# Clustered attention and a bilinear layer on one core: an eleventh sorted pair of heads, and rows that carry their pair's number

## The chip, the core and the metric

The program runs on one core of a Trainium2 chip. A core has five engines with a queue of instructions each: PE (matrix products, into the accumulator memory PSUM), DVE (vector operations), ACT (activations and copies), POOL (here it issues indirect transfers, in which a list of indices says which rows go where) and SP (here it issues plain transfers). Each engine runs its queue in order; they meet through semaphores. The metric is the device time of one execution in microseconds (us).

## The reference

```python
# q, k, v: (4, 8, 768, 64); centroids: (8, 16, 64)
q_assign = argmax(q_n @ c_n.T); k_assign = argmax(k_n @ c_n.T)     # nearest of 16 centroids
mask = q_assign[:, :, :, None] == k_assign[:, :, None, :]
scores = where(mask, scale * q @ k.T, -1e9)
attn = softmax(scores) @ v                                       # (4, 8, 768, 64)
x = attn.transpose(0, 2, 1, 3).reshape(3072, 512)
out = ((x @ w_a) * (x @ w_b)) @ w_out                            # 512 -> 1536 -> 512
```

A query attends only to the keys of its own cluster. The weights arrive as float64 bit patterns and are rounded to float32 in the kernel.

## The kernel before

**Pairs.** Two heads of one batch make a pair; there are 16 pairs, four for each batch, numbered p = 0 to 15. The first `ND` = 6 pairs are *dense*: every score of 768 x 768 is computed, and a large negative term, added by a one-hot product, pushes pairs of other clusters out. A dense pair has 12 units (two halves of queries, six blocks of keys); `score` (line 592) makes the scores of two units, `add_up` (623) sums their exponentials on DVE, `weigh` (634) multiplies them with v, `denominators` (654) and `normalize` finish a half. Pairs 4 and 5 are prepared *by blocks*: DVE turns q and k (514), PE makes similarities (405), DVE makes one-hot rows, and `move_one_hot` (496) moves them with eight transfers.

The other ten pairs are *sorted*, numbered n = 1 to 10 (p = ND + n - 1). Their rows of q, and of k beside v, are written to memory in the order of clusters, so that scores are needed only inside a cluster's strip. A sorted pair passes this chain, written out in `sorted_pair`:

1. *Load* rows (1313) or, for n above `EARLY` = 5, blocks (1324), queries (1332) and keys with values (1338), all on SP.
2. *Turn and assign*: PE transposes (1356) or, late, DVE (1346); similarities (1367) and a prefix count (1404, 1406) on PE; `find`, seven steps on DVE that end in the list of places (1458); `after`, four steps on DVE (1463 to 1472), of which three compute how many rows each cluster strip holds (`in_order`).
3. *Put*: 24 indirect transfers on POOL (1509), 12 of q rows into `qd`, 12 of k and v rows into `kvd`, a ring of five rooms that SP clears with zeros beforehand (`clear`, 1282).
4. *Reload* on SP (1539, 1543), into single buffers `sq`, `sk`, `v`. It waits for the previous pair's values.
5. *Turns* (1552) and *masks* (1557 to 1569) on DVE: from the counts a column of ones and zeros is made beside v, and rows that were not filled are multiplied by zero.
6. *Scores* (1581), exponentials (1592), *values* (1606, 1615), division (1625), and `keep` (1635), which writes the result to memory.
7. *Get*: 12 indirect transfers on POOL (1646), which bring the rows back into the order of tokens; `x_across` (1661) turns them on PE into the input of the bilinear layer.

Pairs 1 to 5 are indexed and put early, while the dense pairs run. Everything from the reload on needs the room that the dense stage leaves (`late_room`, once the dense stage is over and `after` of pair 5 is done).

**The bilinear layer** runs batch by batch. Batch 0's begins beside the last dense pairs, in two blocks of 384 tokens: the up products with `w_a` and `w_b` (727), the product of both on DVE (784), and the down products with `w_out`. Its second block overwrites rows of early pairs, so its first half waits for the puts of pair 3, its second half for those of pair 5. Batches 1 to 3 form all seven products of a two by two split in place of eight; `combine_x` (830) makes differences of x first, other differences (864, 1003, 1014) come in between. A batch's products start only when the last of its four pairs is turned.

**The weights** come in 36 parts: SP loads a part into one of two `raw` buffers (300), DVE rounds it with five instructions (311 to 329), ACT checks it with two (325, 326). The first eight have fixed places, the others are planned by `next_round`.

**The planner.** The order of instructions on each queue is fixed when the program is built, by a planner that keeps a clock for each engine (`Clocked`, with a cost for each kind of instruction) and a heap of due steps. A step of a chain is put off while its engine's clock is ahead of the planned time by more than a limit: `ATT` for turns and masks, `FRONT` for indexing, `LOADS` and `RELOAD` for SP. `paced` ties each indirect transfer to an instruction of PE so that they come `SPACE` apart. `arrived` notes when a weight part is thought to be there.

Of the kernel before, what the change touches and what calls it, by code (L numbers as in the profile page):

```python
# [157 lines left out]
def short_path(nc, tc, ctx, c, cn, centroids_in, casts, n_far, q, k, v,  # L158
# [8 lines left out]
    ND = 2 * HP - 2  # L167
# [5 lines left out]
    SPACE, EARLY, RING = 1.8, 5, 5  # L173
    FRONT, ATT, LOADS, RELOAD = 2.2, 2.8, 1.0, 3.0
# [7 lines left out]
    Gi = Clocked(nc.gpsimd, "G", 1.28, *state)  # L182
    Q_, Qr, Qc = (Clocked(nc.sync, "P", us, *state) for us in (0.42, 0.62, 2.0))
# [9 lines left out]
    counts = pool("counts", 5)  # L193
# [298 lines left out]
    def move_one_hot():  # L492
        while to_move:
            p, ohT, kq, a = to_move.popleft()
            r = 32 * kq + a * NC
            Qr.dma_start(out=ohTs[p][a * D:a * D + NC, kq * HB:(kq + 1) * HB],
                         in_=ohT[r:r + NC, :])
# [258 lines left out]
    def ffn_block(b, blk):  # L756
# [14 lines left out]
        def piece_a(f):  # L771
# [5 lines left out]
            box["h"] = early[blk].rearrange("p (f t) -> p f t", f=NF)  # L777
# [358 lines left out]
    ROWS = 1280  # L1136
    kvd = [dram.tile([2 * ROWS + 32, 2 * D], FP32, name=f"kvd{n}") for n in range(RING)]
# [5 lines left out]
    place = zero.tile([P, 2], FP32, name="place")  # L1143
    order_of = zero.tile([P, NC], FP32, name="order_of")
# [9 lines left out]
    ROW = 2 * NJ * 3 * D  # L1154

    def rooms(rows, qkT, temp, kk):
# [3 lines left out]
        R_["blocks"] = [t[:, 2 * NJ * D:ROW] for t in rows]  # L1160
# [6 lines left out]
    def sorted_constants():  # L1167
# [10 lines left out]
        ints = extra[:, P:P + 32].bitcast(INT32)  # L1178
        nc.gpsimd.iota(ints[:, 0:NC], pattern=[[1, 2], [2, NC // 2]], base=0,
                       channel_multiplier=0)  # L1180
        nc.gpsimd.iota(ints[:, NC:NC + 1], pattern=[[0, 1]], base=0,
                       channel_multiplier=1)
        V.tensor_copy(out=order_of, in_=ints[:, 0:NC])
        V.tensor_copy(out=place[:, 0:1], in_=ints[:, NC:NC + 1])
        Vs.tensor_copy(out=place[0:D, 1:2], in_=place[0:D, 0:1])
        V.tensor_scalar(out=place[D:P, 1:2], in0=place[D:P, 0:1],
                                scalar1=-float(D), scalar2=None, op0=ALU.add)

    def early_room():
        t = hp_.tile([P, NF * HB], FP32, name="h")  # L1190
# [83 lines left out]
    def clear(n):  # L1274
# [3 lines left out]
        def part(i):  # L1278
            t, x, w, m = (kvd[n % RING], 20, 2 * D, 5) if i < 4 else (
# [19 lines left out]
    def sorted_pair(n, start):  # L1299
# [7 lines left out]
        def load_rows(a, second):  # L1307
# [3 lines left out]
                    ((k, kvr[:, a, :, 0:D]), (v, kvr[:, a, :, D:])))[second]  # L1311
# [104 lines left out]
        def index():  # L1416
# [3 lines left out]
            sums, keys = room_[8][:, 0:G], room_[9]  # L1420
# [6 lines left out]
            def totals():  # L1427
# [3 lines left out]
                Vs.tensor_copy(out=keys, in_=total[:, 1])  # L1431
# [20 lines left out]
            def places():  # L1452
# [7 lines left out]
                M["idx"] = idx.rearrange("p (w j a) -> p w j a", w=2, j=NJ)  # L1460

# [7 lines left out]

            def in_order():  # L1470
                M["cnt"] = counts.tile([P, E], FP32, name="cnt_s")
                Vm.tensor_reduce(out=M["cnt"],
                                  in_=cmp.rearrange("p a c d -> p (a c) d"),
                                  axis=AX.X, op=ALU.add)
                mark("after", n)
# [18 lines left out]
                lambda: Vm.tensor_tensor(  # L1494
                    out=cmp, in0=halves(rank_of)[:, :, None, :].broadcast_to(shape),
                    in1=order_of[:, None, :, None].broadcast_to(shape),
                    op=ALU.is_equal),
                lambda: Vm.tensor_tensor(
                    out=cmp, in0=cmp,
                    in1=halves(keys)[:, :, None, :].broadcast_to(shape), op=ALU.mult),  # L1500
                in_order,
# [728 lines left out]
```

## Time and profile before

| What | us |
|---|---|
| median of three runs | 952.77 (952.34 to 955.7) |
| the profiled execution, device time | 951.85 |
| its span, first to last instruction | 950.1 |

The page of the profile gives busy time by engine, the chain of work that ended last, and groups of instructions by source line: output and input by the program's names, shape, count, busy us and mean ns, and the idle time of the engine before them with what ended it. A timeline row has start and duration in us, engine, line, operation, names, and in brackets an idle time before it with its releaser. A row of busy time by window has the window, its length, and for each engine busy us and the number of instructions, then the granted PE clock, the share of the transfer engines, and GB/s. Matmuls overlap at their ends, so the duration of a merged row is a little longer than its distance to the next.

### The profile page before, as it was taken

Reading aid. Unit: us, or ns where it says so; the run is one execution under the profiler, and the core shown is the slowest. Engines: PE = TensorE matmul, PEld = TensorE weight load, DVE = VectorE, ACT = ScalarE, POOL = GpSimd, SP = SyncE. Lnnn points to the kernel's source line nnn. Section 1 sums busy time; section 2 is a strip of 40 time slices with the busy share of each in tenths; the row PEclk is TensorE's granted clock in tenths of the full one; section 3 lists DMA queues with packets and bytes.
Section 4 is the critical chain, followed back from the end, with each engine's and each line's share of the span. In section 5 each row is a group of like instructions: output and inputs, shape, how many; then the busy total and the mean of one; then the engine's idle time right before and its main releaser. Section 6 shows DMA issues by size and latency. Waiting matters only on the chain.

```text
span 950.1 us, 20918 instructions
## 1 busy us (share of the span) xinstructions
PE 928.4 (98%) x8068; PEld 492.4 (52%) x8068; DVE 612.5 (64%) x1309; ACT 261.5 (28%) x564; POOL 372.8 (39%) x373
## 2 busy tenths in 40 slices
PE   8999989999999999999999999999999999999997
PEld 5454433434544567554545676545455664444564
DVE  5899988986869886759575945574354433333542
ACT  5876544633433301122212010212221001211100
POOL 1026645665554564555564545555553200000000
PEclk9999999999999999999999999999999999999999
DMA  8967675556799945784688548383825112122311
GB/s 196 243 177 198 175 219 137 161 172 160 185 218 177 206 145 127 158 179 111 147 150 180 165 98 193 96 184 100 165 55 160 37 57 63 56 61 61 113 35 32
DMA packets 293755, 131.82 MB, mean 139 GB/s; under 512 B 230032, under 2 KB 274832, under 8 KB 293648
## 3 DMA queue, kind: packets, MB, share of 16 engines
q1 hardware_dynamic: 281712, 114.23, 49.2%
q0 software_dynamic: 11520, 15.75, 6.1%
q8 instruction: 66, 1.08, 0.5%
q10 hardware_dynamic: 416, 0.43, 0.1%
q14 instruction: 41, 0.34, 0.1%
HBM read 86.93 MB, written 43.20 MB: 137 GB/s over the span
## 4 chain that ended last, share of the span: by engine, by line
PE 80%; DVE 12%; DMA 3%; SPq 2%; issue 2%; ACT 1%; POOL 0%; DVEq 0%; POOLq 0%; ACTq 0%
PE m L727 64%; PE s L592 3%; PE s L1581 3%; PE s L1606 2%; PE O L634 2%; DVE acc L623 2%; PE s L1615 2%; DVE rest L321 1%; PE s L1661 1%; PE m L405 1%; PE O L1367 1%; DVE rest L318 1%; DMA raw<-in_moe_w_out_dram 1%; PE m L654 1%; PE m L1356 1%
## 5 line engine op out<-in xcount | busy, mean ns | idle before, releaser
L1646 POOL DMA_INDIRECT xT<-od,idx x120 | 123.2, 1027 | 110.1 <-PE m L727 80.8
L727 PE MATMUL m<-xT,wa_sb 128*64 128x384 f32 x672 | 116.6, 488 | 2.2 <-DVE h L784 1.4
L727 PE MATMUL m<-xT,wb_sb 128*64 128x384 f32 x672 | 116.5, 488 | 1.3 <-DVE h L784 1.3
L902 DVE TENSOR_TENSOR ha<-ha,m 128x384 f32<-128x384 f32 x72 | 39.7, 551 | 88.0 <-PE m L727 68.4
L899 ACT COPY h<-m 128x384 f32<-128x384 f32 x72 | 34.4, 478 | 194.6 <-PE m L727 194.6
L727 PE MATMUL m<-wo_sb,h 128*64 128x256 f32 x768 | 87.1, 380 | 0.3 <-DVE wo_sb L329 0.3
L902 DVE TENSOR_TENSOR h<-h,m 128x384 f32<-128x384 f32 x72 | 39.7, 551 | 68.7 <-PE m L727 49.3
L1509 POOL DMA_INDIRECT qd<-whole,idx x60 | 58.6, 976 | 59.9 <-PE m L727 41.6
L727 PE MATMUL m<-raw 128*64 128x384 f32 x432 | 79.2, 487 | 1.0 <-DVE raw L864 1.0
L1509 POOL DMA_INDIRECT kvd<-whole,idx x60 | 58.9, 982 | 53.1 <-PE m L727 34.0
L727 PEld LDWEIGHTS m<-xT,wb_sb 128*64 128x64 f32 x672 | 47.4, 137 | 60.4 <-issue 52.0
L727 PEld LDWEIGHTS m<-xT,wa_sb 128*64 128x64 f32 x672 | 47.2, 137 | 60.1 <-issue 52.1
L727 PEld LDWEIGHTS m<-wo_sb,h 128*64 128x64 f32 x768 | 54.4, 137 | 29.0 <-issue 0.8
L727 PE MATMUL m<-xT,h 128*64 128x256 f32 x576 | 64.4, 379 | 0.0
L1509 POOL DMA_INDIRECT qd<-wo_sb,idx x24 | 27.1, 1128 | 74.5 <-DVE acc L623 59.2
L592 PE MATMUL s<-qkT 64*128 64x384 f32 x288 | 53.1, 487 | 0.0
L727 PE MATMUL m<-xT,size 128*64 128x384 f32 x288 | 52.8, 487 | 0.0
L605 ACT ACTIVATE pt<-s 128x768 f32<-128x768 f32 x58 | 44.9, 809 | 28.1 <-PE s L592 26.7
L727 PEld LDWEIGHTS m<-xT,h 128*64 128x64 f32 x576 | 41.3, 137 | 20.7 <-issue 0.2
L1509 POOL DMA_INDIRECT kvd<-h,idx x36 | 40.4, 1123 | 28.3 <-PE s L592 6.9
L727 PEld LDWEIGHTS m<-raw 128*64 128x64 f32 x432 | 30.8, 137 | 38.9 <-issue 35.7
L899 ACT COPY ha<-m 128x384 f32<-128x384 f32 x54 | 25.9, 479 | 87.2 <-PE m L727 86.4
(270 smaller groups left out, 1530.4 us busy)
## 6 DMA issues: line engine op xcount, KB each, us to landing
whole<-kvd SPq DMA_DIRECT2D x80, 160.0 KB
kvd<-xT SPq DMA_DIRECT2D x20, 320.0 KB
whole<-qd SPq DMA_DIRECT2D x40, 160.0 KB
od<-whole SPq DMA_DIRECT2D x40, 160.0 KB
raw<-in_moe_w_a_dram SPq DMA_DIRECT2D x12, 512.0 KB
raw<-in_moe_w_b_dram SPq DMA_DIRECT2D x12, 512.0 KB
raw<-in_moe_w_out_dram SPq DMA_DIRECT2D x12, 512.0 KB
raw<-up_sums SPq DMA_DIRECT2D x96, 64.0 KB
```

What stands on the lines that cost most here:

```text
L592: ins = nc.tensor.matmul(out=s[:, a, 0:HB], lhsT=Ts[p][r, S + j * P:S + (j + 1) * P], rhs=Ts[p][r, hf * HB:(hf + 1) * HB], start=start, st ...
L605: Sl.activation(out=pt, in_=s[:, :, 0:HB], func=AF.Exp, scale=SCALE)
L623: Vd.tensor_tensor(out=acc, in0=probs[u - 1] if j == 1 else acc, in1=probs[u], op=ALU.add)
L634: ins = nc.tensor.matmul(out=O_of[0][a * D:(a + 1) * D, 0:HB], lhsT=vs[p][:, a, j, :], rhs=probs[u][:, a, :], start=(j == 0), stop=(j == N ...
L727: ins = nc.tensor.matmul(out=ps[half], lhsT=lhsT[:, half], rhs=rhs, **kw)
L899: S_.copy(out=box[name], in_=box["X"][:, 0:HB])
L902: V.tensor_tensor(out=box[name], in0=box[name], in1=box[bank][:, 0:HB], op=ALU.add)
L1509: ins = Gi.indirect_dma_start(out=dst[:, :], out_offset=bass.IndirectOffsetOnAxis(ap=M["idx"][:, w, j, a:a + 1], axis=0), in_=src, in_offs ...
L1581: noted(nc.tensor.matmul(out=tiles[s // 2][r0:r0 + m, s % 2, c0:c0 + m], lhsT=M["skT"][r, h, 32 * x:32 * x + m], rhs=M["sqT"][r, h, 32 * x ...
L1606: noted(nc.tensor.matmul(out=ps[:, s, 65 * i:65 * i + 65], lhsT=pt[:, P * i:P * i + P], rhs=vt[:, i, :], start=True, stop=True))
L1615: noted(nc.tensor.matmul(out=ps[r, s, 65 * (2 + i):65 * (3 + i)], lhsT=pt[r, 2 * P + D * i:2 * P + D * i + D], rhs=vt[r, 2 + i, :], start= ...
L1646: paced(Gi.indirect_dma_start(out=M["xs"][:, j, a * D:(a + 1) * D], out_offset=None, in_=od[n][:, :], in_offset=bass.IndirectOffsetOnAxis( ...
```

## The change

1. `ND` falls from 6 to 5: pair 5 is no longer dense but sorted, and sorted pairs are numbered 1 to 11. Batch 1 has now three sorted pairs instead of two.
2. A row of k and v in `kvd` gets one more float, 129 in place of 128, written with `float(n)` by one memset at the end of `places`. The reload brings this column in beside v, and `filled` turns it into ones and zeros with one comparison against `n`. The counts, three of the four steps of `after`, the constants for them and two of three instructions of `filled` go.
3. `SPACE` falls from 1.8 to 1.55, `ATT` rises from 2.8 to 3.2, and the clears of rooms 2 to 5 are planned earlier.
4. `arrived` is not earlier than SP's clock, and parts below 12 are rounded 7.5 us after it instead of 4.5.
5. The one-hot rows of the by-block pair go out on two queues, SP and ACT, four each.
6. One unit in six, not one in five, uses the borrowed tile for its exponentials; the tile of the second early room is 24 floats wider.

```diff
-    ND = 2 * HP - 2
+    ND = 2 * HP - 3
-    SPACE, EARLY, RING = 1.8, 5, 5
-    FRONT, ATT, LOADS, RELOAD = 2.2, 2.8, 1.0, 3.0
+    SPACE, EARLY, RING = 1.55, 5, 5
+    FRONT, ATT, LOADS, RELOAD = 2.2, 3.2, 1.0, 3.0
+    Qs = Clocked(nc.scalar, "S", 0.1, *state)
...
-            Qr.dma_start(out=ohTs[p][a * D:a * D + NC, kq * HB:(kq + 1) * HB],
-                         in_=ohT[r:r + NC, :])
+            (Qr, Qs)[a].dma_start(
+                out=ohTs[p][a * D:a * D + NC, kq * HB:(kq + 1) * HB],
+                in_=ohT[r:r + NC, :])
...
-        if u % 5 < 4:
+        if u % NJ != 2:
...
-    ROWS = 1280
-    kvd = [dram.tile([2 * ROWS + 32, 2 * D], FP32, name=f"kvd{n}") for n in range(RING)]
+    ROWS, KV, PITCH = 1280, 2 * D + 1, 129
+    kvd = [dram.tile([2 * ROWS + 32, PITCH], FP32, name=f"kvd{n}") for n in range(RING)]
...
+                Vs.memset(M["kvr"][:, :, :, 2 * D], float(n))
...
-            def in_order():
-                M["cnt"] = counts.tile([P, E], FP32, name="cnt_s")
-                Vm.tensor_reduce(out=M["cnt"],
-                                  in_=cmp.rearrange("p a c d -> p (a c) d"),
-                                  axis=AX.X, op=ALU.add)
                 mark("after", n)
...
-                lambda: Vm.tensor_tensor(
-                    out=cmp, in0=halves(rank_of)[:, :, None, :].broadcast_to(shape),
-                    in1=order_of[:, None, :, None].broadcast_to(shape),
-                    op=ALU.is_equal),
-                lambda: Vm.tensor_tensor(
-                    out=cmp, in0=cmp,
-                    in1=halves(keys)[:, :, None, :].broadcast_to(shape), op=ALU.mult),
-                in_order,
...
-                        out=M["v"][:, s, :, 0:D],
-                        in_=kvd[ring][strip(s), D:2 * D].rearrange(
+                        out=M["v"][:, s],
+                        in_=kvd[ring][strip(s), D:KV].rearrange(
                             "(i p) d -> p i d", p=P)), 1)
...
-            Vs.tensor_scalar(out=one_[:, :, 0:2], in0=cnt[:, :, 0:2],
-                              scalar1=place[:, 0:1], scalar2=None, op0=ALU.is_gt)
...
+            Vs.tensor_scalar(out=one_, in0=one_, scalar1=float(n), scalar2=None,
+                              op0=ALU.is_equal)
...
-            arrived[done_to[0]] = clocks["V"] if done_to[0] > 21 else now[0]
+            arrived[done_to[0]] = max(clocks["P"], clocks["V"] if done_to[0] > 21 else now[0])
...
-        if not (i in raws and arrived[i] + (4.5 if i < 22 else 3.5) <= now[0] and may_round(i)):
+        if not (i in raws and arrived[i] + (7.5 if i < 12 else 4.5 if i < 22 else 3.5) <= now[0] and may_round(i)):
...
-        at((0.0, 18.0, 58.0, 92.0, 132.0, 180.0)[n], lambda t, n=n: clear(n))
+        at((0.0, 18.0, 55.0, 90.0, 125.0, 160.0)[n], lambda t, n=n: clear(n))
```

More of the change, by code (lines that the diff above doesn't have):

```diff
@@ L1159, in rooms @@
         R_["kk"] = kk[:, 0:2 * NJ * D].rearrange("p (j a d) -> p j a d", a=2, j=NJ)
-        R_["blocks"] = [t[:, 2 * NJ * D:ROW] for t in rows]
+        R_["blocks"] = [t[:, 2 * NJ * D:2 * NJ * D + 2 * S] for t in rows]
         R_["kvr"] = [t[:, 2 * NJ * D:ROW].rearrange("p (a j d) -> p a j d", a=2, j=NJ)
@@ L1177, in sorted_constants @@
         V.memset(oh, 0.0)
[L1178 to L1187, printed above, removed]
     def early_room():
-        t = hp_.tile([P, NF * HB], FP32, name="h")
+        t = hp_.tile([P, 2 * ROW], FP32, name="h")
         early.append(t)
@@ L1419, in index @@
             rnk, u, h2 = (x.bitcast(INT32) for x in room_[5:8])
-            sums, keys = room_[8][:, 0:G], room_[9]
+            sums = room_[8][:, 0:G]
             halves = lambda x: x.rearrange("p (a c) -> p a c", a=2)
@@ L1707, in sorted_pair @@
         chain += row(FREE, 0.3, later("find", 7), "V")
-        chain += [plan(FREE, 0, lambda: run_chain(row(FREE, 0.2, later("after", 4), "B"), 0.0, start, n))]
+        chain += [plan(FREE, 0, lambda: run_chain(row(FREE, 0.2, later("after", 1), "B"), 0.0, start, n))]
         chain += row(-12, 0.3, [lambda wja=wja: put(*wja) for wja in order], "G",
```

26 lines of the change are left out of this document (7 added, 19 removed).

## The prediction

> **What bounds the kernel now.** I read the page first, then the PE timeline, then busy time by source line, then what its neighbours wait for.
>
> ```profile
> span 950.1 us, 20918 instructions
> PE 928.4 (98%) x8068; PEld 492.4 (52%) x8068; DVE 612.5 (64%) x1309; ACT 261.5 (28%) x564; POOL 372.8 (39%) x373
> PE 80%; DVE 12%; DMA 3%; SPq 2%; issue 2%; ACT 1%; POOL 0%; DVEq 0%; POOLq 0%; ACTq 0%
> ```
>
> PE is idle for 950.1 - 928.4 = 21.7 us in all, so the time is PE's work plus a little. A change gains what it takes from PE, unless PE then waits for something that was hidden behind that work. What is close behind shows in the PE timeline:
>
> ```profile
> 174.79 0.81 PE L654 MATMUL m<-acc,ones 128*64 128x384 f32 x4
> ...
> 203.28 0.81 PE L654 MATMUL m<-acc,ones 128*64 128x384 f32 x4
> ...
> 252.23 2.63 PE L1581 MATMUL s<-whole 32*128 32x128 f32 x128
> ...
> 301.85 2.64 PE L1581 MATMUL s<-whole 32*128 32x128 f32 x128
> ...
> 359.22 2.65 PE L1581 MATMUL s<-whole 32*128 32x128 f32 x128
> ...
> 364.54 0.88 PE L1661 MATMUL s<-ident,xT 128*128 128x128 f32 x6
> ...
> 390.03 2.75 PE L727 MATMUL m<-xT,wa_sb 128*64 128x384 f32 x16
> ...
> 697.54 2.48 PE L1581 MATMUL s<-whole 32*128 32x128 f32 x128
> ...
> 780.52 2.75 PE L727 MATMUL m<-xT,wa_sb 128*64 128x384 f32 x16
> ```
>
> 174.79 and 203.28 are the last denominators of the fifth and sixth dense pair; L1581 the scores of sorted pairs 1, 2, 3 and 10; 364.54 turns the result of sorted pair 2, the last that batch 1's products need; these begin at 390.03 and batch 3's at 780.52. So batch 1's input stands ready 25 us early. Sorted pairs follow one another at 49.6, 57.4 and, from the first to the tenth, (697.54 - 252.23) / 9 = 49.5 us: each is a chain through SP, DVE, PE and POOL over single buffers. That chain is the second bound.
>
> **The pair that moves.** Busy time of L592, L634 and L654 (scores, weighted sums, denominators of all six dense pairs), in this order:
>
> ```profile
> 0.00:206.00 206.00, 65.70 (x432) 30.80 (x432) 0.99 0.68 184
> ...
> 0.00:206.00 206.00, 55.23 (x288) 17.82 (x288) 0.99 0.68 184
> ...
> 0.00:206.00 206.00, 15.14 (x80) 5.38 (x80) 0.99 0.68 184
> ```
>
> 136.1 / 6 = 22.7 us a pair. The sixth pair's similarities are the 129.56 row below, 1.7. Removed: 24.4. The pair comes back as an eleventh sorted one. Five are still indexed early, so the additional one is of the late kind:
>
> ```profile
> L1606 PE MATMUL s<-whole 128*128 128x65 f32 x160 | 22.1, 281 | 0.0
> ...
> L1615 PE MATMUL s<-whole 64*64 64x65 f32 x480 | 18.3, 222 | 0.0
> ...
> L1367 PE MATMUL O<-whole,cTb 128*32 128x192 f32 x80 | 7.8, 518 | 0.0
> ...
> L1406 PE MATMUL O<-oh_s,all_mine 128*128 128x384 bf16 (+5 forms) x30 | 3.7, 259 | 0.0
> ...
> L1404 PE MATMUL O<-oh_s,before_mine 128*128 128x448 bf16 x5 | 1.8, 363 | 0.0
> ```
>
> Scores 2.6 (L1581), values 2.2 + 1.8 over ten pairs, index 1.6 + 0.7 + 0.4 over five, turning 0.9: 10.2 us. PE's work changes by -24.4 + 10.2 = **-14.2 us**.
>
> Elsewhere the move is no saving. On SP 18 issues (loads, values, one-hot rows) become 30 (blocks, queries, keys, reload, result), POOL gets 24 puts and 12 gets more, and DVE exchanges sums and normalising for turns and an index. DVE (64%) and POOL (39%) have room in the mean; what these issues cost, they cost as delay in the chain, below.
>
> **Rounding by SyncE's clock, two queues.** PE's waits near the by-block pairs, ACT's, and SP's issue of the one-hot rows:
>
> ```profile
> 119.82 0.34 PE L592 MATMUL s<-ohT 64*128 64x384 bf16 x2 [2.38 <-ACT pt L605]
> ...
> 129.56 1.70 PE L405 MATMUL m<-qkT,cTb 128*32 128x384 f32 x8 [1.16 <-DVE qkT L514]
> ```
>
> ```profile
> 117.56 0.67 ACT L325 ACTIVATE size<-raw 128x512 f32<-128x512 f32 x1 [1.72 <-DMA raw<-in_moe_w_a_dram]
> ```
>
> ```profile
> 108.19 5.05 SPq L496 DMA_DIRECT2D ohT<-h  x8
> ```
>
> ACT stood at a weight part that had not landed, the exponentials stood behind it, and PE behind them: 2.38 us. A rounding that waits for SP's clock, and 7.5 us more for the first parts, takes this away. The 1.16 belongs to the sixth pair and goes. Together -3.5 us; the bounds are -1.2 and -3.5. Of the eight issues four move to ACT, whose queue then holds them before an exponential: at 5.05 / 8 = 0.6 each +2.5 us at most, -2.5 if SP's half of the wait ends earlier; I take 0, since the fifth pair's scores come groups later. A borrowed tile for one unit in six instead of five, a wider early tile and earlier clears move no work: 0, covered by the next group's PE work.
>
> **POOL, 1.55 apart.**
>
> ```profile
> 62.87 1.15 POOL L1509 DMA_INDIRECT qd<-wo_sb,idx  x1 [59.22 <-DVE acc L623]
> ...
> 281.48 0.96 POOL L1509 DMA_INDIRECT kvd<-h,idx  x1 [0.76 <-DMA whole<-kvd]
> ```
>
> ```profile
> 291.38 2.80 PE L727 MATMUL m<-xT,wa_sb 128*64 128x384 f32 x16 [1.42 <-DVE h L784]
> ```
>
> The 120 early puts kept (281.48 - 62.87) / 119 = 1.84 us for a plan of 1.80. At 1.55 that is 1.58, and the last goes at 62.9 + 119 x 1.58 = 251. Batch 0's second block, which overwrites those rows, reached its second half near 291 and would reach it near 291.4 - 24.4 - 3.5 = 263: covered by 12 us. Had the pace stayed, PE would wait 18.
>
> **Numbered rows.** A copy, three wide DVE instructions and two of three small ones go for each sorted pair, one memset comes:
>
> ```profile
> L1498 DVE TENSOR_TENSOR whole<-whole 128x512 f32<-128x512 f32 x5 | 3.4, 687 | 0.1
> ...
> L1494 DVE TENSOR_TENSOR whole<-whole,order_of 128x512 f32<-128x512 f32 x5 | 3.4, 684 | 0.0
> ...
> L1472 DVE TENSOR_REDUCE cnt_s<-whole 128x32 f32<-128x512 f32 x5 | 3.4, 675 | 0.1
> ```
>
> -2.0 us of DVE a pair, which counts only in the chain of sorted pairs: bounds 0 and -2.0 an interval, taken -2.0, since they stand before the next pair's similarities and among the turns. The memset waits for that room's keys to land and stands before the put that needs it; DVE's h products are queued behind it and PE behind them. Nearest rows are the small DVE ones: 0.2 us, 0 taken.
>
> **Batch 1 now needs three sorted pairs.** This decides the case.
>
> ```profile
> 250.79 10.11 SPq L300 DMA_DIRECT2D raw<-in_moe_w_out_dram  x3
> ...
> 279.15 0.96 SPq L1543 DMA_DIRECT2D whole<-kvd  x2
> ...
> 322.85 2.45 SPq L1543 DMA_DIRECT2D whole<-kvd  x4
> ```
>
> ```profile
> 286.98 0.84 DVE L1552 STREAM_TRANSPOSE whole<-whole 128x640 f32<-128x640 f32 x1
> ...
> 330.41 1.89 DVE L1003 TENSOR_TENSOR xT<-wo_sb 128x512 f32<-128x512 f32 x3
> ...
> 346.21 0.81 DVE L1552 STREAM_TRANSPOSE whole<-whole 128x640 f32<-128x640 f32 x1
> ```
>
> The dense stage ends one pair earlier, 203.3 - 174.8 = 28.5, so pair 1's scores come at 252.2 - 28.5 = 223.7. Pair 2's follow after 49.6 - 2.0 = 47.6. The 57.4 to pair 3 held a collision: its rows were reissued by 325.3, but DVE turned them from 346.2, 20.9 us later, behind the weight differences of batch 0's down products (330.41); for pair 2 that gap was 286.98 - 280.1 = 6.9. Without the collision the interval is 57.4 - 2.0 - 14.0 = 41.4, with all of it 55.4. The down products start 27.9 us earlier too, so the two still meet at the edge, but attention may now queue 3.2 us behind DVE's clock instead of 2.8; I take a quarter of the 14.0, thus 44.9. Pair 3's scores: 223.7 + 47.6 + 44.9 = 316.2. From scores to turned result pair 2 took 364.5 - 301.9 = 62.7; twelve gets 0.25 closer give 59.7, thus 375.9. Then the turning (0.9), the copy and six differences:
>
> ```profile
> L1663 ACT COPY xT<-s 128x768 f32<-128x768 f32 x10 | 8.0, 799 | 26.1 <-PE s L1661 24.4 <-DMA kvd<-whole,idx 1.7
> ...
> L830 DVE TENSOR_TENSOR raw<-xT 128x384 f32<-128x384 f32 x12 | 6.4, 552 | 0.2
> ```
>
> 0.9 + 0.8 + 6 x 0.55 = 5.0, so batch 1's products can start at 380.9. PE is ready for them at 390.0 - 24.4 - 3.5 + 0.9 (one more turning) = 363.0. The gap is 17.9 us. Pair 4's scores and values (2.6 + 2.2 + 1.8) and one late pair's index (2.7), which before lay after 390, fit into it: 9.3. What is lost is **8.6 us**.
>
> **Sum**: 950.1 - 14.2 - 3.5 + 8.6 = 941.0 span. The profiled run took 951.85, 1.75 more: 942.75. The median of the runs, 952.77, is 0.9 above the profiled run: 943.7.
>
> Batch 3: the eleventh scores come at 223.7 + 10 x 47.5 = 699, ready 59.7 + 5.0 later at 763; PE wants them at 780.5 - 24.4 - 3.5 + 10.2 + 8.6 = 771. Covered by 8.
>
> One rule speaks against the change. The Trainium skill, "DMA: Bandwidth & Descriptors", section "How a descriptor splits into AXI transactions", says that a read that does not start at a multiple of 256 bytes also fetches the bytes from the boundary below. Rows of 516 bytes start off it nearly always; by its count 8 beats for a 256-byte piece become up to 16, some 12 in the mean. The kvd half of a reload was issued in 2.45 us, the other alike; half as much again would be an estimate of 2.5 us an interval, 5 on pair 3, and 948 to 949 in the sum. No run here shows it yet.
>
> **The rivals.** *No wait for batch 1* (22%). The sum without the 8.6: 935. For it: 25 us of lead before, and DVE freed in the same stage. Against it: the chain must run three pairs by 371.
>
> *The gain goes into the wait* (18%). The whole collision stays: pair 3's scores at 326.7, products at 391.4, lost 28.4 - 9.3 = 19.1, time 954. The break-even is plain: when batch 1's products start at 390.0, where they did before, the time is 952.8.
>
> *Slower* (13%). On SP, three loads of weights took 10.11 us (250.79), since each waits for DVE to release a buffer, and the next pair's reload stood behind them. All twelve parts of the last weight are now rounded while pairs 2 and 3 reload. One such stop more: products at 401.5, lost 29.2, time 964. It decides from a start at 394.8 on (957.5). Against it: roundings now follow SP's clock.
>
> The forecast itself has 47%, with a range of its own from 939 (half of the 8.6 lost) to 949 (half the collision, and the 2.38 still there).
>
> **How the numbers follow.** About 0.5%, 4.8 us, is what a measurement here can tell from no change: 948.0 to 957.5. Faster: all of no wait and 42 of the forecast's 47, 64%. Same: 18 and the other 5, less 1 for its upper edge, 22%. Slower: 14%. The predicted time is the likeliest, 943.7. The range 933 to 958 reaches below the no-wait case by most of the 2.5 that the two queues could give, and takes in the lost gain.
>
> **What would show it.** PE busy near 914. L1581 first at 224, then at 271 and 316. The third L1661 near 376, and ahead of the first batch-1 product an idle entry of PE, released by DVE or the turning, of some 8 us. The last early put near 251. No ACT wait for a raw weight near 118. Wrong: PE idle of 15 us or more in one place before 400, a second such place before batch 3, or a busy PE above 918.

## The result, and the profile after

| | before | after |
|---|---|---|
| median of 20 runs each, us | 951.84 (950.25 to 955.7) | 956.09 (953.79 to 958.2) |
| ratio after to before | | 1.0044, 95% interval 1.0036 to 1.0052 |
| span of the profiled execution, us | 950.1 | 955.5 |

The change made the kernel 0.44% slower, inside the half per cent that was called no change; the forecast was 943.7. The page after (its line numbers differ a little: 593, 635 and 655 are the dense pairs' lines, 728 the bilinear products, 1548 the scores of a sorted pair, 1573 and 1582 its values, 1628 the turning of its result, 1484 the puts):

```profile
span 955.5 us, 21145 instructions
PE 925.0 (97%) x8145; PEld 495.2 (52%) x8145; DVE 592.3 (62%) x1267; ACT 252.1 (26%) x549; POOL 403.1 (42%) x407
PE 84%; DMA 4%; DVE 3%; POOL 3%; issue 3%; ACT 1%; SPq 1%; POOLq 0%; DVEq 0%; ACTq 0%
```

The span and the mean granted clock of the core, first of the kernel before, then of the kernel after:

```profile
core 0: 950.1 us, clock 0.997
```

```profile
core 0: 955.5 us, clock 0.984
```

PE's busy time fell by only 3.4 us, where 14.2 were expected. The clock explains most of the difference. By the means above 1.6% of 955.5 us are 15.3 us of lost clock after, and 0.3% of 950.1 are 2.9 us before. But a reduced clock lengthens only the work that is done under it, and during part of these times PE stood idle. Summed over windows of 2.5 us, each with PE's busy time in it, the matmuls owe 10.2 us to the clock after and 1.6 before. At full clock PE's work is 925.0 - 10.2 = 914.8 after and 928.4 - 1.6 = 926.8 before: **-12.0 us**, where the forecast had -14.2. On top come **+8.6 us of slow matmuls** and **+8.8 us of idle PE** (30.5 against 21.7). -12.0 + 8.6 + 8.8 = +5.4, which is the difference of the spans. So the work did go, and more than that came back as waits and as slow matmuls.

Where both sit shows in PE's timeline after (start, duration, engine, line, operation, names; the idle time before a row and its releaser in brackets):

```profile
220.45 2.65 PE L1548 MATMUL s<-whole 32*128 32x128 f32 x128
...
260.95 2.65 PE L1548 MATMUL s<-whole 32*128 32x128 f32 x128
...
299.61 2.65 PE L1548 MATMUL s<-whole 32*128 32x128 f32 x128
302.18 0.65 PE L728 MATMUL m<-wo_sb,h 128*64 128x256 f32 x4
304.08 0.65 PE L728 MATMUL m<-wo_sb,h 128*64 128x256 f32 x4 [1.24 <-DVE wo_sb L329]
307.19 1.12 PE L728 MATMUL m<-wo_sb,h 128*64 128x256 f32 x4 [2.46 <-DVE wo_sb L329]
311.08 1.12 PE L728 MATMUL m<-wo_sb,h 128*64 128x256 f32 x4 [2.78 <-DVE wo_sb L329]
314.06 1.97 PE L728 MATMUL m<-wo_sb,h 128*64 128x256 f32 x8 [1.85 <-DVE wo_sb L329]
315.96 1.97 PE L1573 MATMUL s<-whole 128*128 128x65 f32 x8
...
380.22 0.88 PE L1628 MATMUL s<-ident,xT 128*128 128x128 f32 x6
381.02 2.81 PE L728 MATMUL m<-wo_sb,ha 128*64 128x256 f32 x24
383.66 1.46 PE L728 MATMUL m<-xT,wa_sb 128*64 128x384 f32 x8
```

Batch 0's down products begin at 302.18, and from there PE waits four times for DVE's last instruction on a part of `w_out` (329): 1.24 + 2.46 + 2.78 + 1.85 = 8.3 us. From 307 on, four matmuls take 1.12 us where they took 0.65 a row above. Busy time by window (window, length, busy us and number of instructions of PE, PEld, DVE, ACT and POOL, then the granted clock, the transfer engines' share and GB/s) shows the clock:

```profile
302.20:306.90 4.70, 1.29 (x11) 0.38 (x8) 4.49 (x8) 4.42 (x8) 1.74 (x2) 1.00 0.34 99
306.90:314.10 7.20, 2.28 (x10) 0.63 (x10) 6.10 (x12) 3.05 (x7) 0.00 (x0) 0.50 0.30 95
314.10:324.00 9.90, 9.90 (x78) 7.81 (x80) 8.08 (x16) 1.18 (x6) 3.42 (x2) 0.50 0.44 124
324.00:330.00 6.00, 6.00 (x58) 3.90 (x56) 1.87 (x5) 0.31 (x2) 3.85 (x4) 1.00 0.40 98
```

Half the clock for 17.1 us, of which PE was busy for 12.2: 6.1 us of slow matmuls, the largest piece. The last down row above, 314.06, is followed by unbroken work, and still the clock stays at half for 9.9 us more.

The kernel waits for one part after the other because they were rounded one after the other at the very place where they are used. On DVE:

```profile
303.27 0.75 DVE L329 TENSOR_TENSOR wo_sb<-wo_sb,rest 128x512 f32<-128x512 f32 x1
...
306.44 0.69 DVE L329 TENSOR_TENSOR wo_sb<-wo_sb,rest 128x512 f32<-128x512 f32 x1
307.96 0.43 DVE L311 TENSOR_SCALAR wo_sb<-raw 128x512 int32<-128x512 int32 x1 [0.83 <-DMA raw<-in_moe_w_out_dram]
...
310.34 0.69 DVE L329 TENSOR_TENSOR wo_sb<-wo_sb,rest 128x512 f32<-128x512 f32 x1
...
313.32 0.69 DVE L329 TENSOR_TENSOR wo_sb<-wo_sb,rest 128x512 f32<-128x512 f32 x1
```

In the written-out order parts 33, 34 and 35 have no place of their own: they are what `with_weights` still finds in the list and rounds ahead of the first down product (part 32 stands just before). The other waits of PE that count:

```profile
PE m L728 <- DVE wo_sb L329: 8.3, 4, 2.8
PE m L728 <- DMA raw<-up_sums: 5.8, 2, 3.7
PE m L728 <- DVE wa_sb L329: 2.4, 1, 2.4
PE m L728 <- DVE xT L688: 1.3, 1, 1.3
```

The 5.8 are two waits for `up_sums` in batch 2, one just after its start at 585 and one near 686 (batch 3 begins at 785.98 without a wait); the clock is reduced after these too:

```profile
591.47 2.83 PE L728 MATMUL m<-raw 128*64 128x384 f32 x8 [3.67 <-DMA raw<-up_sums]
...
685.83 2.83 PE L728 MATMUL m<-raw 128*64 128x384 f32 x8 [2.18 <-DMA raw<-up_sums]
690.12 1.47 PE L728 MATMUL m<-raw 128*64 128x384 f32 x8
```

Eight matmuls take 2.83 us right after the wait and 1.47 a few rows on.

What the forecast feared did not happen: ahead of 383.66, batch 1's first product, PE does not wait.

### The profile page after: what moved, and what is told of

Same layout as the page of the kernel before. It is cut to its first block, busy times and chain, and to the rows that moved or that the text cites. A ratio compares the mean times of both kernels' runs of the same rounds, so it can differ in the third digit from the quotient of the medians.

```text
span 955.5 us, 21145 instructions
## 1 busy us (share of the span) xinstructions
PE 925.0 (97%) x8145; PEld 495.2 (52%) x8145; DVE 592.3 (62%) x1267; ACT 252.1 (26%) x549; POOL 403.1 (42%) x407
## 4 chain that ended last, share of the span: by engine, by line
PE 84%; DMA 4%; DVE 3%; POOL 3%; issue 3%; ACT 1%; SPq 1%; POOLq 0%; DVEq 0%; ACTq 0%
PE m L728 63%; PE s L593 4%; PE O L635 3%; PE s L1548 3%; PE s L1573 2%; PE s L1582 2%; POOL xT L1613 1%; PE m L655 1%; POOL kvd L1484 1%; PE O L1356 1%; PE s L1628 1%; POOL qd L1484 1%; DMA raw<-up_sums 1%; PE m L389 1%; PE m L1345 1%
## 5 line engine op out<-in xcount | busy, mean ns | idle before, releaser
L1613 POOL DMA_INDIRECT xT<-od,idx x132 | 130.7, 990 | 111.9 <-PE m L728 63.2
L728 PE MATMUL m<-wo_sb,h 128*64 128x256 f32 x768 | 90.3, 388 | 8.3 <-DVE wo_sb L329 8.3
L1484 POOL DMA_INDIRECT qd<-whole,idx x72 | 72.6, 1008 | 59.9 <-PE m L728 37.3
L1484 POOL DMA_INDIRECT kvd<-whole,idx x72 | 71.1, 987 | 46.4 <-PE m L728 30.8
L728 PE MATMUL m<-raw 128*64 128x384 f32 x432 | 82.1, 502 | 5.8 <-DMA raw<-up_sums 5.8
L728 PEld LDWEIGHTS m<-xT,wb_sb 128*64 128x64 f32 x672 | 47.6, 137 | 60.1 <-issue 52.6
L1484 POOL DMA_INDIRECT qd<-wo_sb,idx x24 | 25.0, 1040 | 72.2 <-DVE wo_sb L1449 60.4
L1484 POOL DMA_INDIRECT qd<-h,idx x36 | 37.9, 1054 | 18.4 <-issue 5.2
L1484 POOL DMA_INDIRECT kvd<-h,idx x36 | 38.4, 1068 | 16.9 <-PE m L728 8.0
L593 PE MATMUL s<-qkT 64*128 64x384 f32 x240 | 43.7, 483 | 0.0
```

The costliest lines, as they stand in the source:

```text
L593: ins = nc.tensor.matmul(out=s[:, a, 0:HB], lhsT=Ts[p][r, S + j * P:S + (j + 1) * P], rhs=Ts[p][r, hf * HB:(hf + 1) * HB], start=start, st ...
L728: ins = nc.tensor.matmul(out=ps[half], lhsT=lhsT[:, half], rhs=rhs, **kw)
L1484: ins = Gi.indirect_dma_start(out=dst[:, 0:width], out_offset=bass.IndirectOffsetOnAxis(ap=M["idx"][:, w, j, a:a + 1], axis=0), in_=src, i ...
L1613: paced(Gi.indirect_dma_start(out=M["xs"][:, j, a * D:(a + 1) * D], out_offset=None, in_=od[n][:, :], in_offset=bass.IndirectOffsetOnAxis( ...
```

## The experiments

Runs of one batch share a chip and its runs of the kernel before. On the five chips of these runs the kernel before took 952.05 to 952.17 us (three of them) or 966.15 and 967.06 us (two of them), so only ratios on one chip are compared. Each chip was used for one batch only, so that what belongs to the chip and what to the occasion can't be told apart here. The table has all runs; intervals are 95%.

| kernel | where before takes 952 | where before takes 966 |
|---|---|---|
| changed kernel, r_after | 1.0056 (1.0035 to 1.0078) | |
| the same, r2_after | 1.0043 (1.0027 to 1.0058) | |
| last three parts not rounded, e12 | 0.9897 (0.9881 to 0.9913) | |
| old rounding rule, e1, r_e1, r2_e1 | 1.0107 (1.0082 to 1.0131) | 1.0165 (1.0144 to 1.0187), 1.0133 (1.0113 to 1.0152) |
| 50 matmuls more, e2 | | 1.0235 (1.0210 to 1.0260) |
| six dense pairs, e4, r2_e4 | 1.0028 (1.0016 to 1.0039) | 1.0181 (1.0152 to 1.0209) |
| issues 1.8 apart, e6 | 1.0483 (1.0463 to 1.0503) | |
| before, issues 1.55 apart, e7 | 1.0076 (1.0057 to 1.0095) | |
| before, new rounding rule, e3, r_e3, r2_e3 | 0.9976 (0.9956 to 0.9995) | 0.9927 (0.9902 to 0.9951), 0.9925 (0.9909 to 0.9940) |
| c1 | | 1.0377 (1.0361 to 1.0393) |
| c2, r2_c2 | 0.9955 (0.9935 to 0.9976) | 1.0214 (1.0180 to 1.0247) |
| c3 | 1.0022 (1.0009 to 1.0035) | |

### The last three parts left out

The order is the same instruction by instruction: the planner is charged for the three roundings, they are only not issued. Parts 33 to 35 of `w_out` hold no rounded weights, so the down products' values are not the reference's.

```diff
...
             def with_weights():
                 while rounds:
-                    round_one(rounds.pop(0))
+                    i = rounds.pop(0)
+                    loaded(i)
+                    charge_w(i)
+                    loaded(i + 2)
                 first()
```

> The changed kernel with the same order of everything, but the rounding of the last three parts of w_out (parts 33 to 35, issued ahead of the first down product) left out; the values of those three parts are wrong for it, their loads stay. Theory A: the 8.3 us of waits at the down products shrink to about 1.2 (part 32 stays) and the half clock behind them goes: 10 to 16 us less than the changed kernel beside it. Theory B: it gains under 5, because the time is lost elsewhere.

Beside it the changed kernel itself, with this expectation:

> The changed kernel as it is, so that the runs beside it have it on their own chip (on the chip of the result it stood at 1.0044 of the kernel before; the chip of the four runs so far was some 15 us slower for the kernel before). Theory A (the only new cost of the change is the wait for the last three parts of w_out at batch 0's down products, 8.3 us, and the half clock behind it, 8.5 us): ratio 1.00 to 1.01, whichever chip it is. Theory B (on the slower chip the seven-pair order loses more, in many small waits): 1.015 to 1.025 where the kernel before takes about 967, and 1.004 where it takes about 952.

The changed kernel took 957.53 us, the one without the three roundings **942.20**: 15.3 us less. Its PE timeline (its lines are 8 higher: 736 is the bilinear products, 1581 values, 1636 the turning):

```profile
301.18 0.65 PE L736 MATMUL m<-wo_sb,h 128*64 128x256 f32 x4
302.82 2.38 PE L736 MATMUL m<-wo_sb,h 128*64 128x256 f32 x20 [0.99 <-DVE wo_sb L329]
305.13 1.11 PE L1581 MATMUL s<-whole 128*128 128x65 f32 x8
...
365.71 0.87 PE L1636 MATMUL s<-ident,xT 128*128 128x128 f32 x6
366.51 2.81 PE L736 MATMUL m<-wo_sb,ha 128*64 128x256 f32 x24
369.15 1.46 PE L736 MATMUL m<-xT,wa_sb 128*64 128x384 f32 x8
```

One wait of 0.99 is left, no half clock follows it (eight value products take 1.11 us where they took 1.97), and batch 1's products start at 369.15, again without a wait. Mean clock and PE's busy time, changed kernel first:

```profile
span 955.0 us, 21145 instructions
PE 923.9 (97%) x8145; PEld 494.7 (52%) x8145; DVE 592.0 (62%) x1267; ACT 252.4 (26%) x549; POOL 403.7 (42%) x407
```

```profile
span 938.7 us, 21121 instructions
PE 914.6 (97%) x8145; PEld 490.9 (52%) x8145; DVE 582.8 (62%) x1252; ACT 248.3 (26%) x540; POOL 404.2 (43%) x407
```

PE's idle time falls from 31.1 to 24.1, its busy time by 9.3 with the same number of matmuls. Of the 9.3 the clock accounts for 8.7 (10.4 us of slow matmuls against 1.7, by windows of 2.5 us as above). In the 10.4, 7.5 lie at the down products, and 1.6 after a wait of 2.4 us for a part of `w_a` near 177, which both runs have but which only in r_after was followed by half the clock. So the three late parts cost the change its gain: 7 us as waits and 7 to 8 as slow matmuls.

### The old rounding rule

```diff
-            arrived[done_to[0]] = max(clocks["P"], clocks["V"] if done_to[0] > 21 else now[0])
+            arrived[done_to[0]] = clocks["V"] if done_to[0] > 21 else now[0]
...
-        if not (i in raws and arrived[i] + (7.5 if i < 12 else 4.5 if i < 22 else 3.5) <= now[0] and may_round(i)):
+        if not (i in raws and arrived[i] + (4.5 if i < 22 else 3.5) <= now[0] and may_round(i)):
```

It ran three times. In its order no part is left when the down products begin.

> The changed kernel with the rounding planned as before (a part counts as there at the planned time, 4.5 us of waiting, no look at SP's clock). Theory A (the new rounding rule makes the last parts of w_out late, PE waits 8.3 us for them between 302 and 316 and then runs 17 us at half clock, 8.5 us more): none of the four waits of PE for DVE L329 at the start of the down products, no half-clock stretch near 318, and some 14 to 17 us less than the changed kernel: about 940. Rival B (DVE simply has no room for the rounding once the down products start 24 us earlier): the waits stay above 5 us and the time stays within 4 us of 956. Rival C (batch 1 then waits for its third sorted pair, as forecast): the waits at 302 go, a wait of PE of 8 us or more appears before the first product of batch 1 near 370, and the time lands at 944 to 952.

> The changed kernel with the rounding rule of the kernel before (both clauses undone), once more, on whichever chip this is. In its written-out order no part of w_out is left when the down products begin. Theory D (the new rounding rule is the step that leaves three parts over, and nothing else of it matters): where the kernel before takes about 952, a ratio of 0.988 to 0.995, as with the parts left out; no half clock near 310. Rival (the old rule gives as much back in its own early ACT and PE waits behind raw loads near 120): 1.000 to 1.008.

> The changed kernel with the rounding rule of the kernel before; no part of w_out is left at the down products in its order. Theory D (the rule as planned leaves three parts over, and that is the loss): where the kernel before takes about 952, 0.988 to 0.997. Rival (the old rule's early waits near 120 and a wait of its own at the down products eat it): 1.000 to 1.008. Where the kernel before takes about 966: 1.013 to 1.017, as twice already.

The first two fell on the slower chips, 982.52 and 978.31 us. On the chip of r2_after it took 961.53 against the changed kernel's 956.77: the old rule is not the cure, and the ratio of 1.0107 lies beyond the rival's 1.008 too. Its PE timeline:

```profile
118.87 0.34 PE L593 MATMUL s<-ohT 64*128 64x384 bf16 x2 [2.09 <-ACT pt L606]
...
135.59 1.55 PE L655 MATMUL m<-pt,ones 128*64 128x384 f32 x4 [4.66 <-DVE wo_sb L1374]
...
308.24 0.65 PE L728 MATMUL m<-wo_sb,h 128*64 128x256 f32 x4 [1.39 <-DVE wo_sb L329]
311.68 1.42 PE L728 MATMUL m<-wo_sb,h 128*64 128x256 f32 x8 [2.79 <-DVE wo_sb L329]
313.03 3.80 PE L1548 MATMUL s<-whole 32*128 32x128 f32 x128
```

Two things are seen. There are early waits again: 2.09 us behind the exponentials, as in the kernel before, and 4.66 for the similarities of a sorted pair, which DVE fetched only after a rounding. And at the down products PE still waits, 4.2 us instead of 8.3, although the order has all parts rounded by then. So the new rule is not the whole cause: the down products come some 21 us earlier in this kernel than in the kernel before (305.33 here, 326.39 there), and the last parts cannot keep up under either rule. The new one makes it worse there and better near 120, and taken together it is the better one in this kernel too, by 4.8 us. The traces differ in other waits as well (3.4 us for a sorted pair's turn near 534 with the old rule alone), so what the 4.8 are made of was not shown.

### The rounding rule by itself

The kernel before, with the new rule:

```diff
-            arrived[done_to[0]] = clocks["V"] if done_to[0] > 21 else now[0]
+            arrived[done_to[0]] = max(clocks["P"], clocks["V"] if done_to[0] > 21 else now[0])
...
-        if not (i in raws and arrived[i] + (4.5 if i < 22 else 3.5) <= now[0] and may_round(i)):
+        if not (i in raws and arrived[i] + (7.5 if i < 12 else 4.5 if i < 22 else 3.5) <= now[0] and may_round(i)):
```

> The kernel before with the new rounding rule alone (SP's clock, 7.5 us for the first parts). If the rule is harmful by itself, the last parts of w_out come late here too: PE waits for DVE L329 near 326 and the time rises by 5 us or more. If it hurts only together with the shorter dense stage, the down products of batch 0 begin late enough: no such wait, and the wait of 2.38 us near 119.8 behind ACT goes, so 0 to 4 us less than before.

> The kernel before with the new rounding rule alone. It gained 0.7% on the slower chip. Theory D: where the kernel before takes about 952 it gains the early waits, 3.5 us, and the half clock at 121, 1.7 us: 0.994 to 0.997. Rival (the gain was that chip's): 0.999 to 1.003.

> The kernel before with the new rounding rule alone. It gained 0.75% twice where the kernel before takes about 966. Where it takes about 952: theory D (it saves the early waits of ACT and PE behind raw loads, 3.5 us, and the half clock at 121, 1.7 us): 0.994 to 0.997. Rival (the gain belongs to the slower chips): 0.999 to 1.003. Where it takes about 966: 0.9925 again.

958.48 and 959.34 us against 966 and 967; 948.71 against 952.17. It gains on every chip it ran on: 0.7% on the slower ones, a quarter of a per cent on the other, between that run's two expectations. With six dense pairs the down products come late enough for it: in r2_e3 PE waits 1.15 us for the last part. Where the gain comes from was not shown: the wait of 2.38 us near 120 is gone, but the one of 1.16 for the sixth pair's turned q and k has become 3.54, at 128.48.

### What else the change costs: six dense pairs, issues 1.8 and 1.55 apart

The changed kernel with `ND` as before, all else kept:

```diff
-    ND = 2 * HP - 3
+    ND = 2 * HP - 2
```

> The changed kernel with six dense pairs: all edits but the moved pair. The forecast's terms say that the moved pair takes 14.2 us of PE work away, so this kernel should lie at before's time less the early waits, 948 to 953. If the moved pair is what costs (less slack for rounding and for batch 1), this kernel is the fastest of the four beside the one with the old rounding. If it is slower than before, one of the other edits costs by itself.

> The changed kernel with the third pair of batch 0 left dense (six dense pairs as before), all other edits kept; no part is left at its down products. It tells the moved pair from the rest of the change. Where the kernel before takes about 952: theory E (the other edits cost nothing there; the moved pair is worth some 14 us of PE and loses it again at the down products): 0.995 to 1.003. Rival (the closer issues cost as in the kernel before with 1.55 alone, 0.8%): 1.005 to 1.015. Where it takes about 966: about 1.018 again.

955.54 us beside the changed kernel's 956.77 and the kernel before's 952.13. PE waits for no part of `w_out` in it, and its busy time is 929.3. So the edits around the pair cost 3.4 us by themselves, and the pair adds 1.2: it brings some 14 and loses them, mostly at the down products. The 3.4 are near the sum of the two edits that were tried alone on the kernel before, -3.5 for the rounding rule and +7.2 for the closer issues (below), each beside its own chip's runs.

The changed kernel with the old spacing, and the kernel before with the new one:

```diff
-    SPACE, EARLY, RING = 1.55, 5, 5
+    SPACE, EARLY, RING = 1.8, 5, 5
```

> The changed kernel with its indirect issues 1.8 apart as before, in place of 1.55. Theory C (issues 1.55 apart crowd the DMA queues and so hold up one-hot rows and loads of raw): 8 us or more faster than the changed kernel beside it. Rival, as the prediction had it (the closer issues are what brings batch 1's third pair in time): in the written-out order the FFN list is empty when batch 1 becomes ready, so 5 to 15 us slower, as one wait or a row of fillers near 390.

> The kernel before with its indirect issues 1.55 apart, nothing else. Theory C: 5 to 15 us slower than the kernel before. Rival (the closer issues cost nothing, and bring sorted pairs earlier): within 4 us of it.

With 1.8 the changed kernel takes 997.36 us, 40 more than beside it with 1.55. The rival, that the closer issues are what brings the pairs in time, was right in sign, but far too small and expected in another place. The waits:

```profile
PE O L1356 <- DVE whole L1335: 20.0, 2, 11.6
PE s L1628 <- DMA xT<-od,idx: 18.1, 7, 4.3
```

Two stops, 20.0 us together, come at the similarities of late pairs, whose turns on DVE (1335) stood behind roundings that waited for raw loads (3.7 and 3.9 us). Of the 18.1 us for rows that a get had to bring, 3.8 are the wait for batch 1's third pair, at 398.57, just ahead of that batch's first product: here alone the wait shows that the forecast feared. The other 14.3 are the last pair's, from 806 on: there the chain of sorted pairs is the bound, which no other trace shows. The kernel before needs none of it: with 1.55 it loses 0.76%, 7 us, with waits of 3.8 us behind the exponentials near 120 (2.4 in the kernel before) and 3.7 us for `down_sums` near 540. That theory, that closer issues crowd something, holds in its sign for the kernel before, where what they crowd was not shown, and fails for the changed one.

### Filling the wait

```diff
                 while rounds:
                     round_one(rounds.pop(0))
+                for _ in range(50):
+                    nc.tensor.transpose(out=banks[0][:, 0:P], in_=ident, identity=ident)
                 first()
```

> The changed kernel with 50 transposes of the identity, whose result nobody reads, in PE's queue where the down products of batch 0 begin, so that PE computes while DVE rounds the last parts. Theory A says that the waits cost twice, once as idle time (8.3 us, which stays, now filled) and once as the half clock behind it (17.07 us at 0.5, so 8.5 us): the clock stays at 1.0 in that stretch and the time falls by 6 to 9 us, to 947 to 950. Rival (the half clock has another cause than the idle PE, such as the amount of work): the clock falls to half all the same and the time stays at 956 or rises by the transposes that do not fit the gap, up to 3 us.

It ran on a slower chip, without the changed kernel beside it: 989.70 us. The transposes ran ahead of the waits that were left, 2.4 and 2.3 us; the clock was still full through the first and at half after the second, for 10 us. So the theory that it would stay full was not borne out, but PE was not kept busy either, and nothing follows for the size of the loss.

### Three versions meant to beat both

c1 undoes the arrival clause and rounds parts from 22 on 2.5 after it; c2 undoes the arrival clause and issues 1.5 apart; c3 keeps the clause for 16 parts, rounds the late ones 2.0 after, lets them in at 1.5 us of DVE backlog, and issues 1.5 apart. In all three orders no part is left at the down products.

> A version meant to beat both: the changed kernel with the arrival clause undone (SyncE's clock no longer counts in it) and parts from 22 on rounded 2.5 after that point in place of 3.5. The order has no parts left at the down products, and batches 1 to 3 become ready earlier in it or as early. Theory D: 0.985 to 0.992 of the kernel before. Rival (engines wait behind raw loads that the order takes for landed, up to 10 us spread over 120 to 300): 0.995 to 1.003.

> A second version meant to beat both: the changed kernel with the arrival clause undone and indirect issues 1.5 apart; again no parts left at the down products, batches 1 to 3 ready at 350, 534 and 725 of the written-out order (the changed kernel: 366, 552 and 725). Theory D: 0.985 to 0.992 of the kernel before. Rival (POOL and the DMA queues don't keep 1.5 apart, so that the order is ahead of the chip and PE waits): 1.00 to 1.01.

> The changed kernel as it is, beside the three below. Theory A: about 1.005 where the kernel before takes about 952, as twice already. Theory B: 1.015 to 1.025 where the kernel before takes about 966.

> The changed kernel with the arrival clause undone and issues 1.5 apart, no part left at the down products. Where the kernel before takes about 952, theory D: 0.985 to 0.993; rival (the order runs ahead of the chip, as it did on the slower one): above 1.000. Where the kernel before takes about 966: about 1.02 again.

> A third version meant to beat both: the changed kernel with the arrival clause kept for the first 16 parts (whose waits near 120 it saves) and undone for the later ones, parts from 22 on rounded 2.0 after the planned load in place of 3.5 and let in at 1.5 us of DVE backlog in place of 1.4, issues 1.5 apart. No part is left at the down products; batches 1 to 3 are ready at 363, 559 and 727 of the order. Where the kernel before takes about 952, theory D (early waits and late waits both gone): 0.985 to 0.993. Rival (DVE still ends the last parts late, so that PE waits at the down products in spite of the order): 0.997 to 1.005. Where it takes about 966: 1.01 to 1.02, as all orders with seven sorted pairs there.

c2 took 948.45 us on the chip where the kernel before took 952.13 and the changed one 956.77: 0.45% faster than the one, 0.9% than the other, and less than its theory's 0.7% to 1.5%. It has right values and hardly waits at the down products:

```profile
312.10 1.90 PE L728 MATMUL m<-wo_sb,h 128*64 128x256 f32 x16
314.81 3.67 PE L728 MATMUL m<-wo_sb,h 128*64 128x256 f32 x32 [0.81 <-DVE wo_sb L329]
```

The early waits are there (3.26 us for a sorted pair's similarities, which DVE had yet to fetch, at 132.71). c3 was to have both, and does not: 954.12, as its rival had it. PE waits 3.0 us for a part of `w_out` at the down products, and in a new place,

```profile
257.60 4.37 PE L728 MATMUL m<-xT,wa_sb 128*64 128x384 f32 x16 [6.67 <-DVE h L785]
```

for DVE's h product in batch 0's second half, which stood behind a rounding that waited 10.7 us for its raw load; half the clock follows. On the slower chips c1 and c2 lost 3.8% and 2.1%, as every order with the closer issues did that ran there (1.3 to 3.8%). Neither is a version to keep without trying it on both kinds of chip; the kernel before with the new rounding rule is.

## Why the prediction was wrong

**The failed step** is "the down products start 27.9 us earlier too", in the paragraph on batch 1, which the sum priced at nothing for PE. The prediction used it for DVE's collision with pair 3, but not for the twelve parts of `w_out` that must be rounded by then. The paragraph on rounding by SyncE's clock shares in it: it priced the rule by the wait that it removes (-3.5), and did not ask which parts come later for it, nor when the last of them are needed. But the rule is not the loss itself: with the old one PE still waits 4.2 us at the down products, and the kernel is 4.8 us slower. With the rule and six dense pairs (r2_e4) PE waits for no part of `w_out`. The trace of the kernel before had the rows that show there was no room (on DVE the end of the last part's rounding, on PE the down products):

```profile
327.93 0.69 DVE L329 TENSOR_TENSOR wo_sb<-wo_sb,rest 128x512 f32<-128x512 f32 x1
```

```profile
326.39 1.95 PE L727 MATMUL m<-wo_sb,h 128*64 128x256 f32 x16
328.67 1.52 PE L727 MATMUL m<-wo_sb,h 128*64 128x256 f32 x12 [0.33 <-DVE wo_sb L329]
```

The last part came 0.33 us late already. The deadline moved 24.2 us forward (302.18 against 326.39), the end of the last rounding only 14.6 (314.01 against 328.62), and the difference became waits: 8.3 us, and the half clock behind them, for which the sum had no term either, 6.1 us more (7.5 in r_after). With the parts left out the kernel is at 942.2, 15.3 us less: the missing term is of the size of the whole error, 12.4.

**Right, by the steps.** PE's work: -12.0 at full clock, and -13.9 with the late parts left out (914.6 - 1.7 = 912.9, with 8145 matmuls as in the changed kernel); the forecast was -14.2. The last early put was issued at 248.43 and ended near 250, forecast 251.

**The edits around the pair.** The forecast gave them -3.5 in all: the rounding rule, with nothing for the closer issues beside it. With six dense pairs they measured +3.4. The closer issues alone cost the kernel before 7.2, which the paragraph on POOL did not ask about. In the changed kernel the early waits behind the exponentials went, but 2.4 us for a part of `w_a` at 178 and 1.3 at 125 came in their stead; these are seen in the traces and were not tried apart.

**Batch 1's third pair: wrong in the other direction.** The first scores came at 220.5 (forecast 223.7), the second after 40.5 us (47.6) and the third after 38.7 (44.9): the collision with the down products was gone entirely, since the scores stand before them. The third turning would be at 365.7 without the late parts (375.9). PE reached it at 369 and not at 363, since pair 4's scores and values lay ahead of that point already; what the forecast called filling of a gap was simply work that moved. PE waited for this pair in one run alone, with the issues 1.8 apart, and for 3.8 us, not 8.6. Why the first two intervals were 7 and 6 us shorter than forecast was not tried apart. That e12 lands within 1.5 us of the forecast is therefore in part a chance: 8.6 too much for batch 1, against 6.3 us of waits for `up_sums` and 2.4 for `w_a` in that run that had no term.

**The rivals.** *No wait for batch 1* was right about batch 1 and wrong about the time. *Slower* named the right crowd (all twelve parts of the last weight beside the reloads) but put the loss on SP and on batch 1's start. The sign by which a wrong forecast was to be known, a busy PE above 918, did show: 925.0, though by the clock and not by work that stayed.

**The rule of the Trainium skill** ("DMA: Bandwidth & Descriptors", "How a descriptor splits into AXI transactions") gave an estimate of 5 us for rows off the 256-byte grid. Nothing in the waits answers to it, since pairs 2 and 3 came earlier than forecast, not later. In the trace after, the 260-byte packets of the new reload took 21.1 ns in the mean, those of 256 bytes 22.3, and 19.8 in the trace before.

**Still open.** Why the slower chips punish these orders more was not found. The half clock's share was not tried apart from the wait that precedes it.

## What to carry to other kernels

When work moves earlier, list what it needs and look in the old trace for the smallest wait at its start: a wait of 0.3 us for weights says that there is no slack, and what the consumer moves forward more than its supplier becomes a wait. A rule that delays something to save a stall must be priced at the last thing that it delays, not at the first. And in an order planned with tight clocks the worth of a single edit does not carry over from one kernel to the next: the closer issues cost one kernel 7 us and saved the other 40, and the old rounding rule, which was to cure the late parts, made the changed kernel slower. A fault that a trace shows is priced by leaving out just that work, with the rest of the order kept.

## What the runs showed of the hardware

**Half the clock after short waits, and long after.** No single wait at the down products was over 2.8 us, yet the granted clock fell to 0.50 after 1.24 + 2.46 and stayed there for 17.1 us. The Trainium skill, "TensorE: Matmul & The Clock Gate", in its table under "What's actually happening", has the full clock back after about 3.4 us of sustained work. Here that holds in some places and not in others. In r2_e1, after the waits at 308 and 311, the clock is back by 315.7, after 4.0 us of work (the scores among it). In the changed kernel PE had no gap from 314.1 on, and the clock was at half up to 324.0; in r_after it took longer still:

```profile
314.90:327.60 12.70, 12.70 (x92) 9.38 (x94) 8.28 (x16) 1.50 (x8) 4.51 (x4) 0.50 0.35 99
327.60:333.00 5.40, 5.40 (x54) 3.51 (x52) 2.49 (x5) 0.00 (x0) 3.29 (x4) 1.00 0.55 132
```

What PE ran in that time were mostly the value products of a sorted pair (128 x 65 and 64 x 65) with many weight loads, and in r_after some 4 us of down products after them; whether such small products count less as work was not tried. In e12 the same products ran at full clock. Nor does a wait of one length always have this effect: after 2.42 us near 177 the clock was at 0.66 from 177 to 182 in r_after, and after 2.43 us at the same place in e12 it was at 1.00, on one chip.

**Chips differ.** The same kernel before took 952.05, 952.13 and 952.17 us on three chips and 966.15 and 967.06 on two. This may be the occasion and not the chip, since each was used once. A gain or loss of half a per cent must be measured beside its own reference on the same chip, and may have the other sign on the next: c2 has 0.9955 on one and 1.0214 on another.
